# Attention over 128 heads on one core: a block of K in one load of 64 KB rows, its scores in a rolled loop of eight turns

## The chip, the cores and the metric

The kernel runs on one core of a Trainium2 chip. The metric is device time in microseconds (us) of one execution of the whole program. The engines of a core that matter here are TensorE (PE, with its weight loads listed apart as PEld), VectorE (DVE), ScalarE (ACT), GpSimd (POOL) and SyncE (SP); in this kernel SP does nothing but wait and issue DMAs. Each engine runs its own stream of instructions in order, and they meet through semaphores: an instruction adds to one when it ends, and another engine waits until it has reached a value.

## The reference

```python
B, H, Sq, Skv, Dh = 8, 16, 16, 2048, 256      # all bfloat16
scale  = q.shape[-1] ** -0.5
scores = einsum('bhqd,bhkd->bhqk', q, k) * scale
attn   = softmax(scores, axis=-1)
out    = einsum('bhqk,bhkd->bhqd', attn, v)
```

There are B*H = 128 independent heads, each with 16 queries and 2048 keys and values of 256 numbers. K and V are 134 MB each and are read once; queries and output are 1 MB each.

## The kernel before

**Blocks and slots.** The heads are worked off in G = 16 blocks of 8 heads. A block's K is 8 MB and so is its V: 128 partitions, each with 128 tokens of 512 bytes. One SBUF tensor SL holds four slots of 64 tokens a partition (32 KB): VA and VB together hold the V of a block (VW), KA and KB hold K. A half of K (e = 0 or 1, heads 4e to 4e+3) goes to one slot, one load of 4 MB in rows of 32 KB. V comes in one load of 8 MB in rows of 64 KB (L132). Block 0 has its K in VA and VB, since V is not there yet.

**One block.** TensorE contracts over partitions, so K must stand with its features on them. DVE does that in place, 32x32 blocks at a time, by STREAM_TRANSPOSE at L200 (`kt`): four instructions a block, each over 32 tokens. PE then computes scores (`qk`, L302): for each half e and each pair of 512-column banks, eight feature pairs, one weight load of QW for two matmuls of 512 columns; the second matmul of a pair (L297) uses the weights already loaded. These 64 matmuls a block stand written out in the program. DVE takes the row maximum (L222), ACT the exponential (L282), DVE transposes the probabilities (L226, L227), DVE and ACT copy them into the zero-padded weights PTz (`copies`), and PE multiplies them with V (`pv`, L317): 128 weight loads and 128 matmuls of 256 columns. PE's order is: scores of block r, `SPARE` idle matmuls into X_ps (L297), then `pv` of block r-1. ACT also prepares QW of the next block (`qwb`, L256).

**Rolled and written-out loops.** `nc.Fori` makes a loop in the program: the engine's own sequencer computes addresses and wait values in registers and branches back. The loop over blocks is one on every engine. On PE, inside it, everything is written out except the idle matmuls (L354). The scores of block 0 alone are rolled (L328 to L337): a turn of the inner loop has two weight loads and four matmuls of 512 columns, with addresses taken from registers.

**Who releases what.** SP's order of DMA issues is fixed: K half 0 of block j, K half 1 of block j, V of block j-1. A K half is issued when the scores have used up the slot it goes to (c_qk, L150), V when `pv` of the block before has finished with VW (c_pv, L131). The last two blocks load V in pieces (PIECES), each as `pv` frees its rows. GpSimd works only at the start: it sets zeros and spreads the queries (L184).

Of the kernel before, what the change touches and what calls it, by code (L numbers as in the profile page):

```python
# [5 lines left out]
ALU = mybir.AluOpType  # L6
# [4 lines left out]
SP = mybir.EngineType.SP  # L11
BF16 = mybir.dt.bfloat16
# [3 lines left out]
SPARE = 5  # L16
VA, VB, KA, KB = 0, 1, 2, 3
# [3 lines left out]
def bass_standalone__softmax_full_bidir__sampling_kernel(  # L21
# [16 lines left out]
    ku = k.rearrange("b h s d -> (b h s) d").rearrange("(u p t) d -> u p t d", p=128, t=T)  # L38
# [4 lines left out]
    with ExitStack() as es:  # L43
        ec = es.enter_context
        SL = ec(nc.sbuf_tensor("SL", [128, 4, T, D], BF16))
        QT = ec(nc.sbuf_tensor("QT", [128, SQ * D], BF16))
        QW = ec(nc.sbuf_tensor("QW", [128, 2, 128, 8], BF16))

# [8 lines left out]
        O_all = ec(nc.sbuf_tensor("O_all", [128, G + 2, D], BF16))  # L57
# [8 lines left out]
        def sem(name):  # L66
# [4 lines left out]
        s_k = [sem("s_ka"), sem("s_kb")]  # L71
        s_kl = [sem("s_kla"), sem("s_klb")]
        s_v = sem("s_v")
        s_v0 = sem("s_v0")
# [6 lines left out]
        c_kt = [sem("c_kt0"), sem("c_kt1")]  # L81
# [10 lines left out]

        SLf = SL[:].bitcast(F32)

        QX = PTz[:, 1, 0:SQ * D // 128, :].rearrange("p t m -> p (t m)")

        QXu = QX.rearrange("p (c u a y) -> p a u c y", u=8, a=4, y=2)

        QTu = QT[:].rearrange("p (c u y) -> p u c y", u=32, y=2)

        SLk = SL[:].rearrange("p s (c t) (b i q) -> p s c b q t i", t=16, i=32, q=2)


        PIECES = {last - 1: [(0, 60), (60, 39), (99, 29)],
                  last: [(0, 28), (28, 32), (60, 23), (83, 16), (99, 11), (110, 8), (118, 5), (123, 5)]}

        s_p = {a: sem("s_p%d" % a) for a in sorted({a for w in PIECES for a, n in PIECES[w][1:]})}
        VW = SL[:, VA:VB + 1, :, :].rearrange("p a t d -> p (a t) d")


# [9 lines left out]
        def qx(Q, a):  # L120

            return (QTu[32 * a:32 * a + 32, 8 * Q:8 * Q + 8, :, :].rearrange("p u c y -> p c u y"),
                    QXu[32 * Q:32 * Q + 32, a, :, :, :].rearrange("p u c y -> p c u y"))

        def load_k(eng, g, e, slot, t0, n, s):
            eng.dma_start(SL[:, slot, t0:t0 + n, :], ku[2 * g + e, :, t0:t0 + n, :]).then_inc(s, 16)  # L126

        def on_sync(eng):
            def load_v(w, a, n):

                eng.wait_ge(c_pv, 8 * w + (a + n + C - 1) // C)  # L131
                eng.dma_start(VW[:, a:a + n, :], vb[w, :, a:a + n, :]).then_inc(s_p[a] if a else s_v, 16)  # L132

            eng.dma_start(QX, qh).then_inc(s_q, 16)
            for g, s0, s in ((0, VA, s_k0), (1, KA, s_k)):
                for e in range(2):
                    load_k(eng, g, e, s0 + e, 0, T, s[e])

            for e in range(2):
                eng.wait_ge(c_qk, 4 * e + 4)  # L140
                eng.dma_start(VW[:, T * e:T * e + T, :], vb[0, :, T * e:T * e + T, :]).then_inc(s_v0 if e else s_v, 16)
            for e in range(2):
                eng.wait_ge(c_qk, 4 * e + 12)
                load_k(eng, 2, e, KA + e, 0, T, s_k[e])
            for e in range(2):
                eng.wait_ge(c_pv, 4 * e + 12)
                eng.dma_start(VW[:, T * e:T * e + T, :], vb[1, :, T * e:T * e + T, :]).then_inc(s_v0 if e else s_v, 16)
            with nc.Fori(3, last, engines=[SP], hint_back_edge=True) as j:
                for e in range(2):
# [3 lines left out]
            for e in range(2):  # L153
                eng.wait_ge(c_qk, 8 * last + 4 * e - 4)
                load_k(eng, last, e, KA + e, 0, T // 2, s_k[e])
                load_k(eng, last, e, KA + e, T // 2, T // 2, s_kl[e])
# [4 lines left out]
            eng.dma_start(oh[:, 0:last, :], O_all[:, 2:G + 1, :]).then_inc(s_st, 16)  # L161
            eng.wait_ge(c_ev, G + 1)
            eng.dma_start(oh[:, last, :], O_all[:, G + 1, :]).then_inc(s_st, 16)
            eng.wait_ge(s_st, 32)

        def on_gpsimd(eng):

            for x, n in ([(c_pv, 8)] + [(x, 1) for x in s_kl] +
                         [(s_p[a], 16 * G - 16 * sum(a in dict(PIECES[w]) for w in PIECES)) for a in s_p]):
                eng.sem_inc(x, n)  # L170
            eng.memset(QW[:].rearrange("p e m x -> p (e m x)").bitcast(F32), 0.0).then_inc(c_qt, 1)
            zero = [PTz[:, e].rearrange("p t c -> p (t c)").bitcast(F32) for e in range(2)]
            eng.memset(zero[0], 0.0).then_inc(c_pool, 1)
            eng.memset(mk[:], 1.0).then_inc(c_mk, 1)
            eng.memset(P_sb[:, 0:16], 0.0).then_inc(c_mk, 1)
            eng.memset(P_sb[:, 2064:2080], 0.0).then_inc(c_mk, 1)
            eng.wait_ge(c_mk, 3)
# [10 lines left out]
            eng.wait_ge(c_mk, 7)  # L188
            eng.memset(zero[1], 0.0).then_inc(c_pool, 1)

        def on_vector(eng):
# [6 lines left out]
            def kt(e, h, slot, n=1, first=False):  # L198
# [197 lines left out]
```

## Time and profile before

| | |
|---|---|
| time, median of 3 runs | 631.54 us (631.35 to 631.55) |
| span of the profiled execution, first to last instruction | 630.1 us |
| moved by DMA | 270.54 MB, 429 GB/s over the span |
| busy share of the DMA queue's packets | 99.9% of 16 engines' span |
| busy PE, DVE, ACT, POOL | 535.6, 419.4, 269.1, 26.0 us |
| mean granted TensorE clock | 0.976 |

The profiled execution's own time is its span, 630.1 us; the median of the runs is 1.4 us above it. Times in the profile are counted from the span's start. The busy time of PE counts matmuls that overlap in its pipeline more than once, so 85% does not say that PE has 15% left. A row of the timeline is start, length, engine, line, operation, names, and in brackets the idle time before and what ended it. "PEldq" is the sequencer of PE: its rows (FUSED_REGOPS, several register operations in one instruction; ALU_OP, one; COMPARE_BRANCH, the end of a loop) are not counted as busy, but the view of one source line lists how often each ran and its least, median and greatest length in ns.

### The profile page before, as it was taken

Reading aid. Unit: us, or ns where it says so; the run is one execution under the profiler, and the core shown is the slowest. Engines: PE = TensorE matmul, PEld = TensorE weight load, DVE = VectorE, ACT = ScalarE, POOL = GpSimd, SP = SyncE. Lnnn points to the kernel's source line nnn. Section 1 sums busy time; section 2 is a strip of 40 time slices with the busy share of each in tenths; the row PEclk is TensorE's granted clock in tenths of the full one; section 3 lists DMA queues with packets and bytes.
Section 4 is the critical chain, followed back from the end, with each engine's and each line's share of the span. In section 5 each row is a group of like instructions: output and inputs, shape, how many; then the busy total and the mean of one; then the engine's idle time right before and its main releaser. Section 6 shows DMA issues by size and latency. Waiting matters only on the chain.

```text
span 630.1 us, 7710 instructions
## 1 busy us (share of the span) xinstructions
PE 535.6 (85%) x3336; PEld 273.4 (43%) x2561; DVE 419.4 (67%) x193; ACT 269.1 (43%) x308; POOL 26.0 (4%) x30
## 2 busy tenths in 40 slices
PE   1658989889888898888978889888889878899997
PEld 0112734518244272542726336263362724518386
DVE  1989694865849657496574956749566594768740
ACT  1016562723437243362534525335263352732653
POOL 7800000000000000000000000000000000000000
PEclk9998989999899998999999899999998999999999
DMA  9999999999999999999999999999999999999999
GB/s 377 433 435 431 433 431 424 433 439 426 466 399 466 408 433 441 424 441 424 437 453 408 458 408 458 416 424 441 424 441 449 408 458 408 458 404 421 435 428 376
DMA packets 11008, 270.54 MB, mean 429 GB/s; under 512 B 1024, under 2 KB 3072, under 8 KB 3584
## 3 DMA queue, kind: packets, MB, share of 16 engines
q1 hardware_dynamic: 11008, 270.54, 99.9%
HBM read 269.48 MB, written 1.05 MB: 429 GB/s over the span
## 4 chain that ended last, share of the span: by engine, by line
DMA 57%; PE 34%; issue 4%; DVE 4%; SPq 0%; DVEq 0%; ACT 0%
DMA SL<-in_v_dram 52%; PE O_ps L317 30%; DMA SL<-in_k_dram 5%; DVE SL L200 2%; PE S_ps L296 1%; PE S_ps L297 1%; DVE PTb L227 1%; DVE negm L222 1%; PE X_ps L297 1%; SPq L132 0%; DVE PTz L207 0%; DVE PTz L209 0%; SPq L126 0%; ACT P_sb L282 0%; DVE O_all L247 0%
## 5 line engine op out<-in xcount | busy, mean ns | idle before, releaser
L200 DVE STREAM_TRANSPOSE SL<-SL 128x4096 f32<-128x4096 f32 (+1 forms) x63 | 280.6, 4492 | 88.1 <-DMA SL<-in_k_dram 87.6
L296 PE MATMUL S_ps<-SL,QW 128*128 128x512 bf16 (+1 forms) x512 | 206.1, 403 | 57.6 <-DVE SL L200 48.9
L317 PEld LDWEIGHTS O_ps<-SL,PTz 128*128 128x128 bf16 x2048 | 198.9, 98 | 114.2 <-issue 89.0
L317 PE MATMUL O_ps<-SL,PTz 128*128 128x256 bf16 x2048 | 226.6, 273 | 24.9 <-DMA SL<-in_v_dram 23.8
L297 PE MATMUL S_ps<-SL,QW 128*128 128x512 bf16 (+1 forms) x512 | 205.6, 401 | 0.0
L296 PEld LDWEIGHTS S_ps<-SL,QW 128*128 128x128 bf16 (+1 forms) x512 | 74.4, 145 | 230.1 <-issue 161.9
L256 ACT ACTIVATE QW<-QT 32x256 bf16 x64 | 26.9, 420 | 168.5 <-PE S_ps L297 167.3
L269 ACT ACTIVATE PTz<-PTa 16x1024 bf16<-16x1024 bf16 x32 | 33.8, 1056 | 128.9 <-PE O_ps L317 114.2
L222 DVE TENSOR_REDUCE negm<-S_ps 128x1 f32<-128x2048 f32 x16 | 36.6, 2289 | 58.3 <-PE S_ps L297 58.3
L269 ACT ACTIVATE PTz<-PTa,mk 32x1024 bf16<-32x1024 bf16 x64 | 72.3, 1130 | 0.0
L269 ACT ACTIVATE PTz<-PTb 16x1024 bf16<-16x1024 bf16 x64 | 67.2, 1051 | 1.2
L226 DVE STREAM_TRANSPOSE PTa<-P_sb 128x2048 bf16<-128x2048 bf16 x16 | 37.0, 2312 | 35.4 <-ACT P_sb L282 35.4
L297 PE MATMUL X_ps<-QT,QW 128*128 128x512 bf16 x260 | 58.2, 379 | 0.0
L227 DVE STREAM_TRANSPOSE PTb<-P_sb 128x2080 bf16<-128x2080 bf16 x16 | 36.8, 2302 | 0.0
L269 ACT ACTIVATE PTz<-PTb,mk 32x1024 bf16<-32x1024 bf16 x32 | 36.2, 1132 | 0.0
L282 ACT ACTIVATE P_sb<-S_ps,negm 128x2048 bf16<-128x2048 f32 x16 | 31.5, 1967 | 5.9 <-DVE negm L222 5.9
L262 ACT ACTIVATE O_all<-O_ps,rinv 128x256 f32 x15 | 7.1, 473 | 39.8 <-PE O_ps L317 39.8
L184 POOL COPY QT<-PTz 32x1024 bf16<-32x1024 bf16 x16 | 17.4, 1087 | 2.4 <-DVE PTz L194 1.5
L207 DVE TENSOR_SCALAR PTz<-PTb,mk 32x1024 bf16<-32x1024 bf16 x32 | 15.2, 476 | 0.0
L209 DVE COPY PTz<-PTa 16x1024 bf16<-16x1024 bf16 x32 | 13.5, 422 | 1.1
L247 DVE TENSOR_SCALAR O_all<-O_ps,rinv 128x256 bf16<-128x256 f32 x1 | 0.5, 484 | 20.4 <-PE O_ps L317 20.4
L296 PE MATMUL S_ps<-PTz 128*128 128x512 bf16 x1 | 0.6, 608 | 9.9 <-ACT QW L256 9.9
(18 smaller groups left out, 21.0 us busy)
## 6 DMA issues: line engine op xcount, KB each, us to landing
SL<-in_k_dram SPq DMA_DIRECT2D x30, 4096.0 KB, 24.2
SL<-in_v_dram SPq DMA_DIRECT2D x4, 4096.0 KB, 21.3
SL<-in_k_dram SPq DMA_DIRECT2D x4, 2048.0 KB, 21.5
SL<-in_v_dram SPq DMA_DIRECT2D x1, 3840.0 KB, 21.3
SL<-in_v_dram SPq DMA_DIRECT2D x1, 2496.0 KB, 22.0
SL<-in_v_dram SPq DMA_DIRECT2D x1, 2048.0 KB, 12.2
SL<-in_v_dram SPq DMA_DIRECT2D x1, 1856.0 KB, 24.7
SL<-in_v_dram SPq DMA_DIRECT2D x1, 1792.0 KB, 10.8
```

Source lines behind the costliest of these rows:

```text
L184: eng.tensor_copy(*qx(n // 4, n % 4)).then_inc(c_cq, 1)
L200: eng.transpose(x, x).then_inc(c_k0 if first else c_kt[e], n)
L207: ins = eng.tensor_scalar(out=dst, in0=src, scalar1=m, scalar2=None, op0=ALU.mult)
L222: eng.tensor_reduce(out=negm[:], in_=S_ps[:].rearrange("p c n -> p (c n)"), axis=AX.X, op=ALU.max, negate=True).then_inc(c_mx, 1)
L226: eng.transpose(fa[:, 0:2048], P_sb[:, 16:2064]).then_inc(c_pt, 1)
L227: eng.transpose(fb[:, 0:2080], P_sb[:, 0:2080]).then_inc(c_pt, 1)
L256: eng.activation(dv, src(a), ACTF.Copy, scale=scale).then_inc(c_qw, 1)
L269: eng.activation(dst, src, ACTF.Copy, scale=m if x else 1.0).then_inc(c_co[e], 1)
L282: eng.activation(P_sb[:, 16:2064], sv, ACTF.Exp, bias=negm[:], scale=1.0, accum_out=lsum[:]).then_inc(c_ex, 1)
L296: return eng.matmul(dst, w, x, start=start, stop=stop, skip_group_check=not check)
L297: return eng.add_instruction(mybir.InstMatmult(name=nc.get_next_instruction_name(), engine=PE, start_tensor_calc=start, stop_tensor_calc=stop,
L317: ins = eng.matmul(O_ps[:, 0:D], PTz[:, t // T, t % T, :], VW[:, t, :], start=(t == 0), stop=(t == 2 * T - 1))
```

## The change

**Loads.** K of a block stands in one region KW of 128 tokens. Blocks 2 to 13 load it with one DMA of 8 MB in rows of 64 KB; blocks 1 and 14 in a load of tokens 32 to 127 and one of tokens 0 to 31, block 15 in four loads of 32 tokens. Behind KW lies a new region KX of MV = 32 tokens. In blocks 1 to 14 GpSimd copies tokens 0 to 31 of KW to KX (L200), so that tokens 32 to 127 and then 0 to 31 stand in one row of 128 tokens (KS).

**Scores.** DVE transposes 16 tokens at a time (eight instructions a block instead of four). PE's scores are a rolled loop of eight turns; a turn takes 16 tokens, all 16 combinations of half and feature pair, each with a weight load of its own and one matmul of 256 columns. QW and the scores are laid out to suit. K of block j is issued when six of the eight turns of block j-1 have been counted (c_qk at 8j - 2) and the copy to KX has ended (c_x).

**The rest.** The idle matmuls (three times four now) stand ahead of the scores and wait for K (s_k). ACT prepares QW after the exponential instead of before it. Half of the second copies (`copies(1, (2, 3))`) goes from ACT to DVE, and DVE's first copies stand behind all transposes of the next block. V of block 0 is one load behind all scores of block 0. `pv` takes the tokens in the order 32 to 127, 0 to 31. O_all loses two rows, and QT the columns of block 0.

```diff
+MV = 32
-SPARE = 5
+SPARE = 3
...
+        VW, KW, KX = SL[:, 0:2 * T, :], SL[:, 2 * T:4 * T, :], SL[:, 4 * T:4 * T + MV, :]
+        VS, KS = split(VW), split(SL[:, 2 * T + MV:4 * T + MV, :])
...
-            with nc.Fori(3, last, engines=[SP], hint_back_edge=True) as j:
-                for e in range(2):
-                    eng.wait_ge(c_qk, 8 * j + 4 * e - 4)
-                    load_k(eng, j, e, KA + e, 0, T, s_k[e])
+            with nc.Fori(2, last - 1, engines=[SP], hint_back_edge=True) as j:
+                eng.wait_ge(c_qk, 8 * j - 2)
+                eng.wait_ge(c_x, j)
+                load_k(eng, j, KW, 0, 2 * T, s_k)
                 load_v(j - 1, 0, 2 * T)
...
+            eng.wait_ge(c_qk, 8 * last - 2)
+            eng.wait_ge(c_x, last)
+            for t, x in ((32, s_k), (64, s_kb), (96, s_kc), (0, s_kx)):
+                load_k(eng, last, KW, t, 32, x)
...
+            with nc.Fori(1, last, engines=[POOL]) as n:
+                eng.wait_ge(c_qk, 8 * n)
+                eng.wait_ge(s_k, 16 * n)
+                eng.wait_ge(s_kx, ((n + 2) & 16) + 16)
+                eng.sem_inc(c_mk, 1)
+                eng.tensor_copy(KX.rearrange("p t d -> p (t d)"),
+                                KW[:, 0:MV, :].rearrange("p t d -> p (t d)")).then_inc(c_x, 1)
...
-                    ins = mm(S_ps[:, c, :], QW[:, e, :, bp], SLk[:, slot, c, bp // 2, bp % 2, :, :],
-                             e == 0 and bp == 0, e == 1 and bp == 7, c == cs[0])
+            def qk(dst, x):
+                for e in range(2):
+                    for bp in range(8):
+                        ins = mm(dst, QW[:, e, bp, :], x[:, :, bp // 2, 16 * e:16 * e + 16, bp % 2],
+                                 e + bp == 0, e == 1 and bp == 7, True)
...
-                    for e in range(2):
-                        for h in range(2):
-                            eng.wait_ge(c_kt[e], 2 * r + h - 1)
-                            if e + h == 0:
-                                eng.wait_ge(c_ex, rr)
-                            ins = qk(e, (2 * h, 2 * h + 1), KA + e)
-                        ins.then_inc(c_qk, 4)
+                    with nc.Fori(0, 8, engines=[PE]) as i:
+                        eng.wait_ge(c_qw, 4 * r + 4)
+                        eng.wait_ge(c_kt, 8 * r + i - 7)
+                        qk(S_all[:, bass.ds(256 * i, 256)], KS[:, bass.ds(16 * i, 16)]).then_inc(c_qk, 1)
```

On PE, at the scores of a block, the program before has these rows, from the head of the loop over blocks on ("ISA" is one fused register operation of the sequencer; the last two rows alternate on to 64 matmuls):

```order
L340 BRANCH_PREFETCH_HINT
L340 ISA
L343 COMPARE_AND_BRANCH
L346 ISA
L296 MATMUL S_ps<-SL,QW 128x512 [waits c_ex,c_kt0]
L297 MATMUL S_ps<-SL,QW 128x512
```

and at the same place the changed program has these, a whole turn, but for the further pairs of ISA and MATMUL, all alike, that are left out at the dots:

```order
L370 ISA
L372 ISA [waits c_qw]
L323 ISA [waits c_kt]
L323 ISA
L323 MATMUL S_ps<-SL,QW 128x256
...
L370 REGISTER_ALU
L370 COMPARE_AND_BRANCH
```

So 64 matmuls with constant addresses become eight turns of 16 matmuls, each matmul behind one register instruction: 19 ISA rows, one REGISTER_ALU and one branch a turn.

On SP, in the loop over blocks, the rows before are

```order
L126 ISA [waits c_qk]
L126 DMA SL<-in_k_dram 128x16384
L131 ISA
L132 ISA [waits c_pv]
L132 DMA SL<-in_v_dram 128x32768
```

(the two rows of a K half stand there twice), and in the changed program

```order
L132 ISA [waits c_x,c_qk]
L132 DMA SL<-in_k_dram 128x32768
L138 ISA
L139 ISA [waits c_pv]
L139 DMA SL<-in_v_dram 128x32768
```

One K issue with two waits takes the place of two issues with a wait each; V still stands behind K.

More of the change, by code (lines that the diff above doesn't have):

```diff
@@ L11 @@
 SP = mybir.EngineType.SP
+POOL = mybir.EngineType.Pool
 BF16 = mybir.dt.bfloat16
@@ L145, in on_sync @@
[L145 to L156 removed]
+                load_k(eng, 0, VW, T * e, T, s_k0[e])
@@ L289, in on_scalar @@
                     evac(g + 1)
-                copies(1, (0, 1, 2, 3))
+                copies(1, (0, 1))
         def on_tensor(eng):
@@ L316, in pv @@
                         eng.wait_ge(s_p[t], rr)
-                    ins = eng.matmul(O_ps[:, 0:D], PTz[:, t // T, t % T, :], VW[:, t, :],
+                    ins = eng.matmul(O_ps[:, 0:D], PTz[:, t // T, t % T, :], VW[:, (t + MV) % (2 * T), :],
                                      start=(t == 0), stop=(t == 2 * T - 1))
```

200 lines of the change are left out of this document (107 added, 93 removed).

## The prediction

> **What bounds the kernel now.** I read the page's first line, its queue line and its issue lines first, then the chain that ended last, then SP's timeline.
>
> ```profile
> span 630.1 us, 7710 instructions
> q1 hardware_dynamic: 11008, 270.54, 99.9%
> SL<-in_k_dram SPq DMA_DIRECT2D x30, 4096.0 KB, 24.2
> PTz<-in_q_dram SPq DMA_DIRECT2D x1, 1024.0 KB, 5.0
> out_dram<-O_all SPq DMA_DIRECT2D x1, 64.0 KB, 1.6
> ```
> ```profile
> 505.22 24.23 DMA SL<-in_v_dram
> 529.45 0.23 issue
> 529.68 14.15 PE O_ps L317 x128
> 543.99 24.24 DMA SL<-in_v_dram
> ```
> ```profile
> 505.22 0.33 SPq L132 DMA_DIRECT2D SL<-in_v_dram  x1
> 515.02 8.99 SPq L126 DMA_DIRECT2D SL<-in_k_dram  x2
> 543.99 0.33 SPq L132 DMA_DIRECT2D SL<-in_v_dram  x1
> ```
>
> The 16 DMA engines carry packets all the time: the transfers are the bound. A block's round, V issue to V issue, is 543.99 - 505.22 = 38.77 us for 16.8 MB, so 8 MB take 19.39 us. That is held up only because every issue comes while earlier transfers still run. V lands 24.23 us after its issue, 4.8 more than its own 19.39, and about 1.5 of those are the way to the first byte and from the last (out_dram: 1.6 us for 64 KB, of which 0.15 is transfer; the first load's 5.0 less 2.4 gives at most 2.6). Each K half has more than V: 24.2 us in the page's median against 9.7 of its own. So the question for any change to K is when the issue comes; the rate of rows is second.
>
> **The rows of 64 KB.** Packets are back to back either way, and I can bound what longer rows give from slices that are nearly all K in 32 KB rows (the second and third) against the mixture:
>
> ```profile
> GB/s 377 433 435 431 433 431 424 433 439 426 466 399 466 408 433 441 424 441 424 437 453 408 458 408 458 416 424 441 424 441 449 408 458 408 458 404 421 435 428 376
> ```
>
> 433 and 435 against 433 in a round (16.8 MB in 38.77 us): between half a percent lost and half a percent gained, -3 to +3 us over the run; I take 0. The Trainium skill (DMA: Bandwidth & Descriptors, "Where 436 GB/s comes from") puts the ceiling at 435.2 GB/s; by it a round could fall at most to 38.55 us, an estimate of 3 us gained over the run. The round above is within 0.6% of that, so the page speaks for a small gain at best.
>
> **The moved tokens, DVE and ACT.** The GpSimd copy is 8192 elements a partition, once a block in blocks 1 to 14.
>
> ```profile
> L184 POOL COPY QT<-PTz 32x1024 bf16<-32x1024 bf16 x16 | 17.4, 1087 | 2.4 <-DVE PTz L194 1.5
> L173 POOL MEMSET PTz<- 128x4096 f32 x1 | 3.5, 3515 | 0.0
> L194 DVE STREAM_TRANSPOSE PTz<-PTz 128x2048 f32<-128x2048 f32 x1 | 2.3, 2311 | 5.8 <-DMA PTz<-in_q_dram 5.8
> L200 DVE STREAM_TRANSPOSE SL<-SL 128x4096 f32<-128x4096 f32 x62 | 271.9, 4423 | 87.1 <-DMA SL<-in_k_dram 86.6
> L207 DVE TENSOR_SCALAR PTz<-PTb,mk 32x1024 bf16<-32x1024 bf16 x32 | 15.2, 476 | 0.0
> ```
>
> It costs 3.5 us (a memset of the same bytes) to 8.7 (8 x 1087 ns); I take 8.7, the nearer operation. It starts when K has landed and is wanted after six transposes of 2.31 us, 13.9 us later: hidden, with 5 us over, and if that cover went the excess would be paid each block. Eight transposes of 2.31 are 18.5 us where four of 4.42 were 17.7; with four more copies of at most 0.48 DVE has about 2.7 us more a block, in the wait for K, which in this trace is 87 us in all. ACT gives up as many copies: no cost. SP's second wait (c_x) is met 11 us before its first. V of block 0 as one load waits for all scores of block 0, but the loads ahead of it keep the queue full until about 44 us (5.0 for the queries, then 2 x 19.39): no cost.
>
> **The rolled scores.** This is the step that I think decides. The scores of block 0 are rolled in the kernel before, so the trace has a price. PE's timeline, then the sequencer's rows by source line from 28.4 to 42.9 us (ten turns), then the loop of the idle matmuls (L354):
>
> ```profile
> 28.92 0.44 PE L296 MATMUL S_ps<-SL,QW 128*128 x1 [0.35 <-issue]
> 29.19 0.38 PE L297 MATMUL S_ps<-SL,QW 128*128 x1
> 29.41 0.38 PE L296 MATMUL S_ps<-SL,QW 128*128 x1
> 29.63 0.38 PE L297 MATMUL S_ps<-SL,QW 128*128 x1
> 30.33 0.44 PE L296 MATMUL S_ps<-SL,QW 128*128 x1 [0.32 <-issue]
> ```
> ```profile
> L296 PEldq FUSED_REGOPS  x30: 102/138/143, 28.5 to 42.2; - x30
> L296 PEldq ALU_OP  x10: 36/36/36, 29.2 to 42.4; - x10
> L300 PEldq FUSED_REGOPS  x20: 51/51/51, 28.9 to 42.5; - x20
> L330 PEldq FUSED_REGOPS  x10: 50/50/50, 28.4 to 41.6; - x10
> L330 PEldq ALU_OP  x10: 32/32/32, 29.5 to 42.6; - x10
> L330 PEldq COMPARE_BRANCH  x10: 76/208/215, 29.6 to 42.7; - x10
> L354 PEldq ALU_OP  x5: 36/36/36, 403.9 to 405.6; - x5
> L354 PEldq COMPARE_BRANCH  x5: 79/220/222, 404.0 to 405.7; - x5
> ```
>
> A turn takes 30.33 - 28.92 = 1.41 us, though its four matmuls start 0.22 us apart, 0.88 in all: PE waits for "issue", its own sequencer. The nine register rows of a turn last 2 x 0.138 + 0.12 (the third row of L296, between its least and its median) + 2 x 0.051 + 0.050 + 0.036 + 0.032 + 0.208 = 0.82 us; the other 0.59 are gaps, 0.066 a row, two weight loads and four matmuls inside. The changed turn has 21 such rows: 4 at its head (50, 51, 138 and some 41 ns by their like), 15 of 51, one of 36, one branch of 208, in all 1.29 us, and 21 gaps of 0.066 are 1.39: 2.67 us. It also has 16 weight loads and not 2 for every 9 rows, 11 too many for that gap. They cost 0 to one gap each (0.73 us). So a turn is 2.67 to 3.40 us; the rows do not separate the ends, and I take the middle, 3.0. PE itself would want 16 x 0.11 = 1.77 (14.15 us for 128 pairs at L317), and DVE hands over a chunk every 2.31. The sequencer becomes the slowest of the three.
>
> The Trainium skill (TensorE: Matmul & The Clock Gate, "Wait — 56ns, not 53.3ns?") says that with hardware decode off the sequencer spends about 62 ns on each MATMUL. The idle loop does not agree: four matmuls and two register rows take some 0.41 us there, and the two rows with their gaps are 0.036 + 0.22 + 0.13 = 0.39 of it.
>
> **What the turns delay.** K of the next block is now issued after the sixth turn. The way from one turn's last matmul to the issue is in these rows:
>
> ```profile
> 398.12 0.38 PE L297 MATMUL S_ps<-SL,QW 128*128 128x512 bf16 x1
> ```
> ```profile
> 398.68 8.99 SPq L126 DMA_DIRECT2D SL<-in_k_dram  x2
> ```
>
> 0.56 us; with 256 columns some 0.5. From K's landing to the next K's landing: first chunk transposed 2.4; six turns of 3.0 less 0.6 for the rows at a turn's edge that lie before the first wait and after the last matmul, 17.4; to SP 0.5; to the first byte and from the last 1.5; transfer 19.4. Sum 41.2 against 38.8: the queue runs dry and 2.4 us are lost in each of the 12 rounds from K of block 2 to K of block 14, some 29 us. The point at which the round is no longer lengthened is a turn of 2.6 us (38.8 = 23.2 + 6 x 2.6). V's issue also comes late (scores end 26.4 after K's landing, pv 14.15 later, 41 in all) but within the longer round, so it costs nothing beside.
>
> ```profile
> 99.14 4.32 PE X_ps L297 x20
> 627.21 0.05 issue
> ```
>
> The end: V of block 0 lands at 64 (44 + 19.4 + the way) and K of block 2 at 83.7, if its issue just meets the queue's end; I estimate so, and a us later there is a us in the result. Eleven rounds of 41.2 bring K of block 13 to 536.9; issue of K of block 14 20.3 later, its first 96 tokens land 16 us on, at 573.2. Scores of 14: 2.4 + 24. Idle matmuls 12 x 0.216 (4.32 us for 20) = 2.6, pv of 13 14.15, scores of 15 another 24 (their K is long there): 640.3. The first rows of V of block 15 are free after 32 tokens of pv, 3.5; then 1.5 + 19.4 for its pieces, and 2.9 from the last landing to the end (627.2 to 630.1): 667.6. Plus 1.4 from span to median: **669 us**. For the ends, 2.67 gives 639 and 3.40 gives 704 by the same sum.
>
> **Rivals.**
> 1. The register rows are hidden (the sequencer gets ahead while PE still works, or a weight load covers them). Then turns follow the transposes, K's round is 2.4 + 5 x 2.31 + 1.8 + 0.5 + 1.5 + 19.4 = 37.1, under 38.8, and the time stays at 631, give or take the 3 us of the row length. For it: no row shows 16 loads each behind a register row, so the sum of single rows may be too much. Against it: the issue gaps at every turn of the rolled loop quoted.
> 2. Faster: the turn is below 2.6 us and the rows of 64 KB gain over half a percent of the transfer; it takes 1.3 us of its 3 to be outside 0.2%, which is about what a measurement of this kernel tells from no change. 629. Against it: 433 and 435 with short rows already.
> 3. The turn lies only just above 2.6: 633 to 638, from two or three hundredths of a us a row.
> 4. GpSimd's copy takes over 14 us, if it and DVE's transposes hinder each other; DVE then waits, and each us over some 20 (where six slow turns end, and SP waits for c_x) adds 12 us: at 22 us, 690. No row shows the two together.
> 5. Every matmul also costs the sequencer a gap of 0.066: a turn of 3.0 + 1.06, and 12 x 6 + 16 turns of 1.06 more than the forecast, 762. The idle loop speaks against it, as said. This is the direction of the rule of the Trainium skill's page on TensorE named above.
>
> **How the numbers follow.** The forecast (a turn of 2.67 to 3.40, 639 to 704) 0.66; rival 1 0.16; rival 2 0.06; rival 3 0.05; rival 4 0.04; rival 5 0.03. Slower: 0.66 + 0.05 + 0.04 + 0.03 = 0.78; same 0.16; faster 0.06. Predicted is the forecast's 669, its own range 639 to 704. The range for 8 in 10 leaves out rival 2, 4 and 5 in part and the forecast's far end, and takes in rival 1: 630 to 692.
>
> **What would show it.** Right: matmuls at L323 in steady blocks start some 0.13 to 0.16 us apart, turns 3.0 us, with idle put down to issue; the DMA share falls to about 94% and the mean rate to some 405 GB/s (270.54 MB in 668 us); V and K land about 21 us after their issue, since nothing is ahead of them; DVE's transposes end before the turns; POOL shows 14 copies of some 8.7 us ending before their transposes. Wrong: turns of 2.3 to 2.4 that wait for DVE, a DMA share that stays at 99.9%, K landing over 23 us after its issue; or POOL copies over 14 us with DVE waiting on them.

## The result: 680.5 us, 7.7% slower

The changed kernel takes 680.5 us (median of 5 runs, 677.65 to 681.13) beside 631.43 us for the kernel before on the same chip (5 runs, 631.19 to 631.55): a ratio of 1.0769, 95% interval 1.0754 to 1.0785. The forecast was 669.0. The profiled execution has a span of 677.7 us, 47.6 more than before.

Lines of the page after; the first of the groups is the score matmuls (L323), the second the new GpSimd copy:

```profile
span 677.7 us, 12610 instructions
...
DMA  8998999999989999899989998998999999999968
GB/s 371 464 402 371 433 414 391 402 398 429 422 348 410 402 406 433 371 429 375 422 383 433 426 379 371 433 433 371 429 375 422 398 418 387 406 398 437 414 254 303
...
q1 hardware_dynamic: 8992, 270.54, 95.2%
...
L323 PE MATMUL S_ps<-SL,QW 128*128 x1984 | 279.3, 286 | 86.1 <-issue 48.8
...
L200 POOL COPY SL<-SL 128x8192 bf16<-128x8192 bf16 x14 | 98.2, 7015 | 465.5 <-DMA SL<-in_k_dram 465.5
...
L280 ACT ACTIVATE QW<-QT 32x256 bf16 x60 | 80.3, 1338 | 1.1
```

The bytes are the same, the DMA share fell from 99.9% to 95.2%, and the eights in the DMA line stand all along the span: the loss is paid round by round. SP's timeline, where each row is the issue of one transfer (the line L132 loads K, L139 loads V):

```profile
397.06 0.33 SPq L132 DMA_DIRECT2D SL<-in_k_dram  x1
417.37 0.33 SPq L139 DMA_DIRECT2D SL<-in_v_dram  x1
438.26 0.33 SPq L132 DMA_DIRECT2D SL<-in_k_dram  x1
458.53 0.33 SPq L139 DMA_DIRECT2D SL<-in_v_dram  x1
479.24 0.33 SPq L132 DMA_DIRECT2D SL<-in_k_dram  x1
```

A round from K issue to K issue is 41.2 and 41.0 us here, 41.5 in the mean of all twelve (64.69 to 562.99), where the round was 38.77. The issue list of the trace, with the median time to landing, says that almost nothing is queued ahead of a transfer any more (both were 24.2):

```profile
SL<-in_v_dram SPq DMA_DIRECT2D x14, 22.7
SL<-in_k_dram SPq DMA_DIRECT2D x12, 22.0
```

And the chain that ended last shows what the K issue waits for: turns of 16 matmuls, each followed by 0.61 to 0.67 us in which TensorE's own sequencer is between turns, and then the load of K:

```profile
430.15 2.23 PE S_ps L323 x16
432.38 0.61 issue
432.99 2.23 PE S_ps L323 x16
435.22 0.67 issue
435.88 2.22 PE S_ps L323 x16
...
438.26 21.75 DMA SL<-in_k_dram
```

A turn is 432.99 - 430.15 = 2.84 us. By the issue rows of V of block 2 and V of block 13 (117.60 and 543.99 us before, with the end at 630.1; 126.31 and 583.29 after, with the end at 677.7) the 47.6 us fall into three parts: 8.7 up to the first of the two, 30.6 in the eleven rounds between them (41.54 against 38.76), and 8.3 behind the second.

### The profile page after: what moved, and what is told of

It is laid out like the page before. It is cut to its first block, busy times and chain, and to the rows that moved or that the text cites. A ratio compares the mean times of both kernels' runs of the same rounds, so it can differ in the third digit from the quotient of the medians.

```text
span 677.7 us, 12610 instructions
## 1 busy us (share of the span) xinstructions
PE 552.0 (81%) x4212; PEld 391.0 (58%) x4032; DVE 447.3 (66%) x315; ACT 257.7 (38%) x240; POOL 122.5 (18%) x43
## 3 DMA queue, kind: packets, MB, share of 16 engines
q1 hardware_dynamic: 8992, 270.54, 95.2%
## 4 chain that ended last, share of the span: by engine, by line
DMA 47%; PE 23%; DVE 18%; issue 11%; DVEq 0%; SPq 0%; ACT 0%; ACTq 0%
DMA SL<-in_k_dram 47%; DVE SL L212 17%; PE S_ps L323 16%; PE O_ps L347 6%; PE X_ps L324 0%; DVE PTa L241 0%; SPq L132 0%; DVE PTb L242 0%; DVEq L264 0%; DVEq L257 0%; DVEq L265 0%; DVE O_all L271 0%; ACT O_all L287 0%; SPq L145 0%; ACTq L287 0%
## 5 line engine op out<-in xcount | busy, mean ns | idle before, releaser
L323 PE MATMUL S_ps<-SL,QW 128*128 x1984 | 279.3, 286 | 86.1 <-issue 48.8
L212 DVE STREAM_TRANSPOSE SL<-SL 128x2048 f32<-128x2048 f32 (+1 forms) x120 | 278.0, 2382 | 102.3 <-DMA SL<-in_k_dram 102.3
L323 PEld LDWEIGHTS S_ps<-SL,QW 128*128 128x128 bf16 x1984 | 191.7, 97 | 247.6 <-issue 184.3
L200 POOL COPY SL<-SL 128x8192 bf16<-128x8192 bf16 x14 | 98.2, 7015 | 465.5 <-DMA SL<-in_k_dram 465.5
L280 ACT ACTIVATE QW<-QT 32x256 bf16 x60 | 80.3, 1338 | 1.1
L294 ACT ACTIVATE PTz<-PTa,mk 32x1024 bf16<-32x1024 bf16 x32 | 36.2, 1131 | 0.0
L294 ACT ACTIVATE PTz<-PTb 16x1024 bf16<-16x1024 bf16 x32 | 33.5, 1048 | 0.4
L221 DVE COPY PTz<-PTb 16x1024 bf16<-16x1024 bf16 x32 | 13.5, 421 | 4.7 <-PE O_ps L347 3.7
L189 POOL COPY QT<-PTz 32x1024 bf16<-32x1024 bf16 (+1 forms) x16 | 15.7, 981 | 3.1 <-DVE PTz L206 2.1
L219 DVE TENSOR_SCALAR PTz<-PTa,mk 32x1024 bf16<-32x1024 bf16 x32 | 15.2, 476 | 0.0
## 6 DMA issues: line engine op xcount, KB each, us to landing
SL<-in_v_dram SPq DMA_DIRECT2D x1, 3840.0 KB, 17.9
```

What stands on the lines that cost most here:

```text
L200: eng.tensor_copy(KX.rearrange("p t d -> p (t d)"), KW[:, 0:MV, :].rearrange("p t d -> p (t d)")).then_inc(c_x, 1)
L212: eng.transpose(x, x).then_inc(s, n // 16)
L219: ins = eng.tensor_scalar(out=dst, in0=src, scalar1=m, scalar2=None, op0=ALU.mult)
L280: eng.activation(dv, src(a).rearrange("p e (q b) y -> p e q b y", b=4), ACTF.Copy, scale=scale).then_inc(c_qw, 1)
L294: eng.activation(dst, src, ACTF.Copy, scale=m if x else 1.0).then_inc(c_co[e], 1)
L323: return eng.matmul(dst, w, x, start=start, stop=stop, skip_group_check=not check)
```

## The experiments

The theory to be tested: a rolled turn of 2.84 us on TensorE's sequencer, together with one load of K that can only be issued behind the sixth turn, empties the DMA queue. Each ratio is to the kernel before on the same chip (medians of 631.27 to 631.48 us in the four sets). Every time is a median, with the lowest and highest run in brackets.

### One half undone at a time

The turns written out, everything else left:

```diff
-                    with nc.Fori(0, 8, engines=[PE]) as i:
-                        eng.wait_ge(c_qw, 4 * r + 4)
-                        eng.wait_ge(c_kt, 8 * r + i - 7)
-                        qk(S_all[:, bass.ds(256 * i, 256)], KS[:, bass.ds(16 * i, 16)]).then_inc(c_qk, 1)
+                    eng.wait_ge(c_qw, 4 * r + 4)
+                    for i in range(8):
+                        eng.wait_ge(c_kt, 8 * r + (i - 7))
+                        qk(S_all[:, 256 * i:256 * i + 256], KS[:, 16 * i:16 * i + 16]).then_inc(c_qk, 1)
```

> Only the form of the score loop goes back: the eight turns of a block are written out with constant addresses; K stays one load of 64 KB rows, the GpSimd copy stays, DVE still transposes 16 tokens at a time. Theory (the rolled turn of 2.84 us on PE's sequencer makes the round too long): without register rows a turn takes 16 x 0.11 = 1.8 us and follows the transposes of 2.2 us; landing to K issue falls from 19.3 us to about 15.3, a K round would be 37.0 us, below the 38.8 of the transfers, the queue stays full: 630 to 636 us. Rival B (one load for the whole of K is issued and waited for too late, whatever the turns): K issues stay 41 us apart, 670 to 681 us. Rival C (packets of 64 KB are slower, 2498 ns in the mean against 2 x 1210): V and K still land 21.8 us after issue with nothing ahead of them, over 650 us. Rival D (the copy and the 16-token transposes hold DVE up): over 650 us with DVE late in each block.

641.75 us (637.34 to 644.25), ratio 1.0183 [1.0167, 1.0200]. 38.8 us of the 49 come back, so the rolled form was needed for the loss, and rival B as the whole cause falls; C and D were to give over 650 us and fall too. But 10 us stay, 6 more than the theory allowed. (The traced run is the fastest of the five, 637.34 us: what is read from this trace below covers the first 6 of the 10 us.) The number of register rows at L323 on TensorE's sequencer, after and here:

```profile
L323 PEldq FUSED_REGOPS  x2108: 42/46/94, 19.8 to 644.6; - x192
```
```profile
L323 PEldq FUSED_REGOPS  x68: 46/46/80, 19.9 to 36.0; - x68
```

The other half, on SP: turns stay rolled, K of a block comes in three loads.

```diff
-            with nc.Fori(2, last - 1, engines=[SP], hint_back_edge=True) as j:
-                eng.wait_ge(c_qk, 8 * j - 2)
-                eng.wait_ge(c_x, j)
-                load_k(eng, j, KW, 0, 2 * T, s_k)
-                load_v(j - 1, 0, 2 * T)
+            for j in range(2, last):
+                eng.wait_ge(c_x, j)
+                eng.wait_ge(c_qk, 8 * j - 4)
+                load_k(eng, j, KW, MV, 64, s_k)
+                eng.wait_ge(c_qk, 8 * j - 2)
+                load_k(eng, j, KW, MV + 64, 32, s_kc)
+                load_k(eng, j, KW, 0, MV, s_kx)
+                load_v(j - 1, 0, 2 * T)
```

> The opposite half: the turns stay rolled (2.84 us each), but K of a block comes in three loads: tokens 32 to 95 are issued after the fourth turn, 96 to 127 after the sixth, 0 to 31 right behind them (SP's list is written out, with constant waits). Theory: the turn hurts only by way of the issue that waits for the sixth turn. Now the first 64 tokens are issued 2.7 + 4 x 2.84 - 0.5 = 13.6 us after they landed, while 9.7 us of K and V are still queued; the queue stays full and the round is 38.8 us: 631 to 640 us (the last scores and the idle matmuls still cost some us at the end). PE has 22.7 + 14.15 + 0.7 = 37.6 us of work in a round, just under 38.8. Rival F (PE is itself the bound with the rolled turns, through V's issue behind pv): rounds stay at 41 us, 665 to 681 us.

644.05 us (643.80 to 644.52), ratio 1.0202 [1.0186, 1.0217]: 36.5 us come back with every turn still at 2.84, and the time is 4 us above the theory's range. So neither half does the whole harm alone. Two rows of V's issue in SP's timeline, eleven rounds apart:

```profile
122.45 0.33 SPq L139 DMA_DIRECT2D SL<-in_v_dram  x1
...
548.46 0.33 SPq L139 DMA_DIRECT2D SL<-in_v_dram  x1
```

38.73 us a round: rival F (TensorE as the bound) falls. The 12.9 us that the span still has over before lie outside these rounds: 4.85 ahead of the first row, nothing between, 8.4 behind the second. If that reading holds, it must be enough to write out the turns of blocks 1, 14 and 15:

```diff
+                    mid = eng.to_reg((r + 14) & 15)
+                    with eng.If_lt(mid, last - 3):
+                        with nc.Fori(0, 8, engines=[PE]) as i:
...
+                    edge = eng.to_reg((r + 2) & 15)
+                    with eng.If_lt(edge, 4):
+                        eng.wait_ge(c_qw, 4 * r + 4)
+                        for i in range(8):
...
```

> The split load with rolled turns, but the turns of blocks 1, 14 and 15 written out; blocks 2 to 13 stay rolled at 2.84 us a turn. Theory: with K issued after the fourth turn the rolled turns cost nothing in steady rounds (38.85 us there), and the 12.7 us that the split form lost lie at the start (4.8 us at the second V issue) and in the tail (8 us, two blocks of scores of some 22 us in a row with nothing to hide them): 631 to 635 us. If the rolled turns cost in the steady rounds too: over 640 us.

634.53 us (634.40 to 635.43), ratio 1.0049 [1.0034, 1.0065], within the expected range. Twelve blocks of rolled turns cost almost nothing once K's issue does not wait for six of them (V's rounds are 38.85 us, from 118.43 to 545.81); the start and the end, where nothing hides them, cost 9.5 us.

### Doses

Four of the eight turns rolled:

```diff
-                    with nc.Fori(0, 8, engines=[PE]) as i:
+                    with nc.Fori(0, 4, engines=[PE]) as i:
...
+                    for i in range(4, 8):
+                        eng.wait_ge(c_kt, 8 * r + (i - 7))
+                        qk(S_all[:, 256 * i:256 * i + 256], KS[:, 16 * i:16 * i + 16]).then_inc(c_qk, 1)
```

> A dose: the first four turns of a block stay rolled, the last four are written out. Theory: turns 4 and 5 take 1.8 us each instead of 2.84 (their transposes are done by then), so landing to K issue is 2.7 + 11.4 + 3.6 + 0.15 = 17.8 us instead of 19.3 and the round 39.5 instead of 41.1: 0.7 us lost in each of 12 rounds in place of 2.75, plus a shorter end (two blocks of scores 3 to 4 us shorter each): 636 to 648 us, between the written-out and the rolled form. If instead any register loop in the block throws away the same time (a fixed price for entering it): as in the rolled form, over 665 us. If rows hide: no different from the written-out form.

653.55 us (651.86 to 655.21), ratio 1.0355 [1.0335, 1.0375]: between the two forms as the theory has it, 5.5 us above its range.

Every second weight load left out of the rolled turns:

```diff
-                                  e + bp == 0, e == 1 and bp == 7, True)
+                                  e + bp == 0, e == 1 and bp == 7, bp % 2 == 0)
```

> Rolled as in the changed kernel, but every second weight load is left out (its matmul uses the weights of the one before, so the scores are other numbers): 16 register rows and 16 matmuls stay, 8 loads go. It prices what a load costs the sequencer. Theory (the rows set the pace, a load adds about 0.02 us as the raw starts show): the turn falls by 0.15 to 0.2 us to 2.65 to 2.7, K's round by six of these to some 40.0: 662 to 668 us. Rival (each load costs a gap like a row's, 0.066 us): the turn falls by 0.53 to 2.3, below 2.6, and the queue stays full: 635 to 642 us.

671.09 us (666.93 to 674.02), ratio 1.0616 [1.0575, 1.0657], 3 us above the theory's range. Starts of two turns that follow each other in TensorE's timeline:

```profile
422.21 0.28 PE L323 MATMUL S_ps<-SL,QW 128*128 x1 [0.61 <-issue]
...
424.92 0.28 PE L323 MATMUL S_ps<-SL,QW 128*128 x1 [0.66 <-issue]
```

A turn of 2.71, 0.13 less for eight loads: 0.016 us a load. The rival's 0.066 is out, so it is the register rows, those of the turn's edge above all, that set the pace: in the changed kernel the first and the last of a turn's 16 matmuls start 1.95 us apart, where 15 x 0.11 would be 1.65, and from the last start to the next turn's first are 0.89. Of the 1.07 us that a turn has over 16 x 0.11 = 1.77, 0.3 lie between the pairs and 0.8 at the edge.

Four turns of 32 tokens, so that one register row stands for a matmul of 512 columns:

```diff
-                    with nc.Fori(0, 8, engines=[PE]) as i:
+                    with nc.Fori(0, 4, engines=[PE]) as i:
                         eng.wait_ge(c_qw, 4 * r + 4)
-                        eng.wait_ge(c_kt, 8 * r + i - 7)
-                        qk(S_all[:, bass.ds(256 * i, 256)], KS[:, bass.ds(16 * i, 16)]).then_inc(c_qk, 1)
+                        eng.wait_ge(c_kt, 8 * r + 2 * i - 6)
+                        qk(S_all[:, bass.ds(512 * i, 512)], KS[:, bass.ds(32 * i, 32)]).then_inc(c_qk, 2)
```

> The changed kernel, still rolled and with one load of K, but in four turns of 32 tokens (matmuls with 512 columns) in place of eight of 16: half the register rows a token. Theory (register rows are paid per matmul): a turn is 16 x 0.216 = 3.46 us of TensorE, more than 16 pairs at 0.124, so rows inside a turn are hidden and only its edge, some 0.6 us, shows: 4.1 us for 32 tokens, below the 4.4 of their two transposes. K is issued after the third turn: 4.5 (two transposes) + 2 x 4.4 + 3.5 + 0.15 = 17 us after the landing if the clock holds, a round of 38.8; but TensorE idles some 4 us before K lands, so the clock may be at 0.5 for the first turn (as in the written-out form), some 2 us a round: 633 to 655 us. If the loop itself (a turn's head and branch), not the rows per matmul, made it slow: some 2.84 + 1.77 = 4.6 us a turn, 660 us or more.

655.18 us (653.95 to 657.86), ratio 1.0390 [1.0371, 1.0410], at the upper end. The price a token is as expected: the turns now wait for DVE and start 4.39 us apart, though they are still a loop.

```profile
418.14 3.64 PE L323 MATMUL S_ps<-SL,QW 128*128 x16 [0.39 <-DVE SL L212]
422.53 3.64 PE L323 MATMUL S_ps<-SL,QW 128*128 x16 [0.74 <-DVE SL L212]
426.92 3.64 PE L323 MATMUL S_ps<-SL,QW 128*128 x16 [0.75 <-DVE SL L212]
```

### The clock, a second theory

In the written-out form TensorE stands idle 5.2 us before K lands, and the idle matmuls that follow run slowly. The first row here is of TensorE's timeline. The last two are stretches of the round before it, where the gap was 5.16 us: length, busy us of PE, PEld, DVE, ACT and POOL with the number of instructions, granted clock (1.00 is full speed), DMA share, GB/s. The granted clock is 0.50 in the first stretch and 1.00 in the second.

```profile
437.71 4.26 PE L324 MATMUL X_ps<-QT,QW 128*128 128x512 bf16 x12 [5.20 <-DMA SL<-in_k_dram]
```
```profile
398.80:402.00 3.20, 3.12 (x8) 0.00 (x0) 3.20 (x2) 0.88 (x1) 2.87 (x1) 0.50 0.76 328
403.60:418.30 14.70, 14.44 (x129) 12.00 (x127) 14.61 (x11) 0.00 (x0) 2.55 (x1) 1.00 0.99 428
```

That the clock halves when TensorE idles is what the Trainium skill says (TensorE: Matmul & The Clock Gate, "HAM oscillation — how this bites in real kernels": idle gaps of more than about 3.4 us between bursts of matmuls), and the trace agrees at 5.2 us. The theory was that this made up the missing 10 us. The written-out form with 24 idle matmuls that don't wait for K:

```diff
-                    with nc.Fori(0, SPARE, engines=[PE]) as x:
+                    with nc.Fori(0, 2 * SPARE, engines=[PE]) as x:
                         eng.wait_ge(c_cq, 16)
-                        eng.wait_ge(s_k, r16)
                         spare()
```

> The written-out form again, with the idle matmuls no longer waiting for K: 24 of them (for 12) run straight behind the matmuls with V and fill the 5.2 us in which TensorE stood idle before K landed. Theory (of the 10.4 us that the written-out form still lost, most is the clock: after 5.2 us of idleness the granted clock was 0.50, the 12 idle matmuls took 4.3 to 5.3 us instead of 2.75 and turn 0 came 2 to 2.5 us after its chunk was ready): the clock stays at 1.00, turn 0 follows its transpose 2.4 us after the landing, K is issued 15 to 16 us after the landing, the queue is never dry, rounds are 38.8 us: 631 to 635 us. Rival (64 KB packets are slower by themselves: 425 GB/s at a DMA share of 99.4%): no change from the written-out form, 637 to 644 us.

639.16 us (634.72 to 645.88), ratio without the run of 645.88 1.0111 [1.0083, 1.0140]. The mean granted clock rose from 0.930 to 0.979, and at best a quarter of the 10 us was won; the runs of the two forms overlap. The two profiles say why: from DVE's first transpose of K to the next K's issue were 15.8 us cold and are 15.4 warm, because written-out turns of 1.8 us catch up on transposes of 2.2. The theory fell for this form. The rival's number came true; that 64 KB packets are slower by themselves did not, as the section on the seam shows.

The same edit in the rolled form, first with 12 idle matmuls, then with 20:

```diff
                         eng.wait_ge(c_cq, 16)
-                        eng.wait_ge(s_k, r16)
                         spare()
```

> The changed kernel with one edit: the 12 idle matmuls no longer wait for K and run straight behind the matmuls with V (a gap of some 1.8 to 2.1 us before K lands). It prices the clock's part in the rolled form. Theory: the rounds of 42.1 to 42.5 us (idle matmuls at a granted clock of about 0.5, 4.1 to 4.4 us of them) disappear, and the others lose the 0.3 us by which 12 idle matmuls outlast the first transpose: 12 rounds of 40.8 in place of a mean of 41.5, 8 to 9 us less: 670 to 673 us, with less scatter. If the clock has no part in it: 677 to 681 us.

678.75 us (678.47 to 680.49), ratio 1.0750 [1.0734, 1.0765].

```diff
-                    with nc.Fori(0, SPARE, engines=[PE]) as x:
+                    with nc.Fori(0, 5, engines=[PE]) as x:
                         eng.wait_ge(c_cq, 16)
-                        eng.wait_ge(s_k, r16)
                         spare()
```

> The changed kernel with 20 idle matmuls in place of 12, not waiting for K: 4.3 us, which fills the gap before K lands (1.8 to 2.1 us) and the first transpose (2.3 us). With 12 of them nothing was won, since they ended before or soon after the landing and TensorE then stood idle 2.0 to 2.6 us and began the first two turns cold. Theory (the clock has a part of its own in the rolled form): no cold turns, rounds of 40.7 to 41.0 in place of 41.5: 670 to 675 us. If the part of the clock is nothing: 677 to 681 us.

679.68 us (679.42 to 680.53), ratio 1.0769 [1.0753, 1.0786], and with it the granted clock is 0.995 in the mean. Nothing was won that these runs can tell from the changed kernel's 677.65 to 681.13 us: in all three rolled traces first transpose to issue is 19.2 us a round. The timeline of the run with 12 idle matmuls that do not wait for K shows why, in the first four turns of a block:

```profile
380.15 2.64 PE L323 MATMUL S_ps<-SL,QW 128*128 x16 [2.02 <-DVE SL L212]
383.03 5.11 PE L323 MATMUL S_ps<-SL,QW 128*128 x32 [0.23 <-issue]
388.75 2.23 PE L323 MATMUL S_ps<-SL,QW 128*128 x16 [0.61 <-DVE SL L212]
```

Where the matmuls are slow, the gap of 0.61 us behind a turn shrinks to 0.23 or to nothing, and three turns take 388.75 - 380.15 = 8.60 us, where three warm ones take 8.52. So the sixth ends at nearly the same time, and these runs show no part of the clock in the 49 us.

It has one where V is what the round waits for. Both halves undone (the two edits shown first, together), with the idle matmuls where the change puts them:

```diff
-            with nc.Fori(2, last - 1, engines=[SP], hint_back_edge=True) as j:
+            for j in range(2, last):
...
-                    with nc.Fori(0, 8, engines=[PE]) as i:
+                    for i in range(8):
```

> Both halves undone: turns written out, and K in three loads (tokens 32 to 95 after the fourth turn, the others after the sixth). Still changed: 16-token transposes and turns, the GpSimd copy, V of block 0 in one load, the layout of the query weights. Theory (the rest of the change costs nothing): 631 to 634 us, and DMA share 99.8% or more, rounds of 38.8. If copy, transposes or layout cost something by themselves: over 637 us.

641.89 us (640.89 to 642.92), ratio 1.0162 [1.0147, 1.0177], 8 us more than expected. The chain there is V, the matmuls with V, the next V, and a stretch of 3.45 us at their start (columns as above) has half the clock:

```profile
356.70 22.71 DMA SL<-in_v_dram
379.41 0.14 issue
379.55 17.02 PE O_ps L346 x128
```
```profile
379.55:383.00 3.45, 3.45 (x17) 2.47 (x18) 3.30 (x2) 3.40 (x4) 0.00 (x0) 0.50 0.99 427
```

17.02 us for what takes 14.15 at full clock. The idle matmuls taken from ahead of the turns and put back behind them, 20 in blocks 2 to 14:

```diff
-                with eng.If_lt(rr, last):
-                    with nc.Fori(0, SPARE, engines=[PE]) as x:
-                        eng.wait_ge(c_cq, 16)
-                        eng.wait_ge(s_k, r16)
-                        spare()
...
-                    with eng.If_eq(rr, last - 1):
-                        with nc.Fori(0, SPARE, engines=[PE]) as x:
+                    mid = eng.to_reg((r + 14) & 15)
+                    with eng.If_lt(mid, last - 2):
+                        with nc.Fori(0, 5, engines=[PE]) as x:
                             spare()
```

> Split load and written-out turns as in the run that lost 10.6 us, and the 20 idle matmuls of a block put back to where the kernel before has them, behind the scores and ahead of the matmuls with V (none ahead of the scores). Theory: what was left there is the clock alone: with fast scores the place where TensorE waits is in front of V (5.6 to 6.9 us), the matmuls with V then began cold and took 15.6 to 17.0 us in place of 14.15, and the chain V, matmuls with V, next V was that much longer. Filled with 4.3 us of idle matmuls the clock holds: V rounds of 38.8 us, matmuls with V of 14.15, 631 to 634 us. If 16-token transposes, the GpSimd copy, the layouts or loads cost something beside: it stays over 636 us.

634.56 us (634.32 to 634.95), ratio 1.0049 [1.0035, 1.0063]: 7.3 us less. Matmuls with V are at full clock again:

```profile
453.84 14.13 PE L346 MATMUL O_ps<-SL,PTz 128*128 128x256 bf16 x128 [0.26 <-DMA SL<-in_v_dram]
```

So everything else in the change (copy, 16-token transposes, layouts, V of block 0 in one load) costs some 3 us together, 0.6 more than expected; which of it was not tried. By V's issue rows (118.87 for block 2, 545.91 for block 13, a span of 633.6) 1.3 us of the span's 3.5 lie at the start, 0.7 in the eleven rounds and 1.6 in the end. No version run beats the kernel before.

### The copy

GpSimd's copy made twice in a row:

```diff
+                for h in range(2):
+                    eng.wait_ge(c_mk, 6 + (n - 1) + h)
                     eng.tensor_copy(KX.rearrange("p t d -> p (t d)"),
-                                KW[:, 0:MV, :].rearrange("p t d -> p (t d)")).then_inc(c_x, 1)
+                                    KW[:, 0:MV, :].rearrange("p t d -> p (t d)")).then_inc(c_x if h else c_mk, 1)
```

> The changed kernel with GpSimd's copy of the 32 tokens made twice in a row (the second over the first), 14 us in place of 7.0, so that it ends about when the seventh transpose is due, 15 to 16 us after K's landing. Theory (the copy is hidden under six rolled turns, 19.2 us): 678 to 682 us, no change. Rival (copy and transposes hinder each other, or DVE waits for the copy with consequence): each us that the seventh transpose is pushed past turn six adds to the end of the scores and, past 19.2 us, to K's issue: over 684 us, and DVE's transposes beside the copy longer than 2.27 us.

680.59 us (679.77 to 682.17), ratio 1.0787 [1.0769, 1.0805], beside 680.5: no change. The two groups of this trace (by shape):

```profile
L213 DVE STREAM_TRANSPOSE SL<-SL 128x2048 f32<-128x2048 f32 x114 | 253.4, 2280 | 112.4 <-DMA SL<-in_k_dram 94.3 <-POOL SL L201 18.1
...
L201 POOL COPY SL<-SL 128x8192 bf16<-128x8192 bf16 x28 | 196.4, 7013 | 374.5 <-DMA SL<-in_k_dram 373.7
```

DVE now waits 18.1 us for the copies, and it is hidden under the slow turns; transposes beside 14 us of copying take 2280 ns, 2274 in the changed kernel.

### What was missing in the theory: the seam between two transfers

All kernels with one load of K were slower than the sum said. Per round, in us, worked out from the issue rows, from DVE's first transpose of each K, and from the trace's packets. "Packets late" is how much longer than their usual time (2.42 us for 64 KB) the packets of one DMA engine took in a round, "engine empty" how long it had no packet; both are means over the 16 engines. The first six rows are means of the twelve rounds from K of block 2 to K of block 14, the last two of eleven rounds of V:

```
kernel                   issue to     transpose    round    packets   engine
                         transpose    to issue              late      empty
changed                  22.3         19.2         41.5     1.30      1.49
half the loads           22.85        18.35        41.2     1.29      1.30
four turns rolled        22.95        17.3         40.2     0.71      0.81
turns of 32 tokens       23.1         17.3         40.5     0.84      0.92
written out              23.35        15.8         39.2     0.41      0.05
written out, warm        23.9         15.4         39.3     0.54      0.06
split, rolled            (three loads)             38.7     0.0       0
before                   (two loads)               38.8     0.05      0
```

In every row the last two columns together are what the round has over 38.8 us, to within 0.2. So in the changed kernel the empty queue, which was forecast, is about half of the 2.8 us lost in a round; the other half is packets that take longer.

The sum took the round as the greater of 38.8 and 21 + the second column, a sharp corner at 17.9. The corner is round: at 17.3 the round is already 1.5 us too long, at 15.4 0.5, and only with a load issued well ahead does the excess go. Of the late time, 88 to 99% is in packets that start within 3 us of the point where one transfer follows the other. In the changed kernel the first 16 packets of a transfer take 3.1 us in the median (the middle half of them 2.9 to 3.2).

In these traces the lateness goes with how long before the end of the transfer ahead the next one is issued; no run varied that alone. From the same packets, in us, the mean of each kernel's twelve seams of a kind, with the least and the greatest lead:

```
kernel, transfer         issued ahead by      late at the seam
changed, K               0.0 (-1.6 to 0.8)    0.68
changed, V               0.9 (0.8 to 1.0)     0.62
written out, K           1.9 (0.4 to 2.7)     0.30
written out, warm, K     2.2 (1.4 to 2.8)     0.44
turns of 32 tokens, V    3.0 (2.8 to 3.6)     0.13
written out, V           3.5 (2.8 to 3.9)     0.06
```

So what stays of the loss in the written-out form lies at the seam ahead of K, which is issued some 2 us ahead; V, issued 3.5 us ahead, follows with almost none. Why a packet takes longer at the seam was not tried and stays open.

## Why the prediction was right, and where its terms were off

- **The mechanism** is the one forecast: turns set by the sequencer, K's issue behind the sixth, the queue empty, a longer round for each block. Each half undone alone brings 36 to 39 us of the 49 back. The rivals fall: rows hidden, and faster (the turns wait for "issue" and the result is slower); a turn just above the threshold (2.84 against 2.6); the copy (7.0 us, and 14 cost nothing); another gap for each matmul (2.84, not 4.06). On this last the rule of the Trainium skill that it cited (TensorE: Matmul & The Clock Gate, "Wait — 56ns, not 53.3ns?") shows as no further cost a matmul: a pair of load and matmul starts every 0.124 us with its 46 ns row. Whether the 62 ns that the rule names lie within the 0.124 us these runs do not tell.
- **The turn**: 3.0 predicted, 2.84 measured. The middle was taken between loads that cost nothing and loads that cost a gap each; measured, a load costs 0.016 us, a quarter of a gap, so the lower end was nearer: 2.67 and 11 loads at 0.016 make 2.85. Inside a turn the matmuls start 0.124 us apart, where 0.13 to 0.16 was said.
- **K's round**: 41.2 predicted, 41.5 measured, by two errors that cancel, so the close number is luck. From landing to issue the sum had 20.3 (2.4 + 17.4 + 0.5), measured 19.2; from issue to landing it had 20.9, measured 22.3 (both up to and from DVE's first transpose). The second is the mis-sized step from issue to landing. By the packets, the 22.3 are 1.1 to an engine's first packet, 19.4 of transfer, 0.7 of late packets at the seam, 0.8 by which the last of the 16 engines ends behind the middle one, and 0.3 to the transpose: the "1.5 to the first byte and from the last" held, and the late packets and the uneven end were missing beside it. The threshold of 2.6 us worked out from it is therefore not one.
- **The start**: K of block 2 was to land at 83.7 "if its issue just meets the queue's end; a us later there is a us in the result". It did not meet it: V of block 0 ended at 63.30, K of block 2 was issued at 64.69, and no packet ran until 65.65. Its first transpose starts 22.05 us after the issue, at 86.74: 3.0 us too late.
- **The end** was mis-sized by about 5 us. TensorE's timeline of the changed kernel:

```profile
609.14 14.14 PE L347 MATMUL O_ps<-SL,PTz 128*128 128x256 bf16 x128
623.11 1.94 PE L323 MATMUL S_ps<-SL,QW 128*128 x16
...
645.45 14.13 PE L347 MATMUL O_ps<-SL,PTz 128*128 128x256 bf16 x128 [0.46 <-issue]
660.59 14.13 PE L347 MATMUL O_ps<-SL,PTz 128*128 128x256 bf16 x128 [1.00 <-ACT O_all L287]
```

  The sum let the last V's pieces set the end (3.5 + 1.5 + 19.4 + 2.9 = 27.3 from the start of the matmuls with V of block 14). In fact TensorE waits for no V there (the last piece lands at 672.4, its matmuls come at 674.2), and two blocks of matmuls with V run in a row with an evacuation between: 677.7 - 645.45 = 32.2. Together: 3.0 at the start, 4.0 in eleven rounds (41.56 against 41.2), -1.2 from K of block 13 to the issue of the next, 0.9 in that load, -1.5 in the scores and matmuls up to 645.45, 4.9 behind: the 10.1 us between the forecast span of 667.6 and 677.7.
- **The copy**: 8.7 predicted (eight small copies), 7.0 measured, hidden as said. **64 KB rows**: taken as 0, and a packet in the middle of a transfer takes 2.42 us as two of 32 KB took 2.43; what the long single loads cost beside the empty queue is the seam. **DVE and ACT**: hidden as said.

## What to carry to other kernels

A rolled loop with register addresses has a price a matmul (here 0.124 us for a pair that TensorE does in 0.11, plus 0.8 us at a turn's edge), and it shows only where a transfer is issued behind it, or at the start and the end, where nothing hides it: look first at which transfer waits for the loop, and split that transfer, before unrolling. A loop on the sequencer stops setting the pace when each row carries more work (with 512 columns in place of 256 the turns followed DVE, though the kernel was still 3.9% slower than before). When a DMA-bound kernel is summed up, don't take a transfer that is issued just in time as free; count it as late until it is issued well before the one ahead of it ends (here some 3.5 us).

## What the runs showed of the hardware

- **Packets are slower at the seam**: 3.1 us in the median for the first 64 KB packets of a transfer that was issued less than 1 us before the one ahead of it ended (changed kernel), 2.42 in mid-transfer. Issued 3.5 us ahead, the seam lost 0.06 us (written out, V).
- **The clock can fall after a shorter gap than expected.** In the rolled form with 12 idle matmuls ahead of K, TensorE stood idle 2.63 us before 422.18, and the stretch behind has:

```profile
422.20:424.50 2.30, 2.30 (x13) 1.59 (x14) 2.30 (x2) 0.00 (x0) 2.30 (x1) 0.62 1.05 456
```

  The Trainium skill's 3.4 us (TensorE: Matmul & The Clock Gate, "HAM oscillation — how this bites in real kernels") is longer than this gap; the measurement decides: 0.62 is the granted clock behind 2.63 us of idleness.
- **ScalarE's copy of the query weights** takes 1338 ns in the new layout (L280 above). The group in the page of before, for the same 32x256 elements:

```profile
L256 ACT ACTIVATE QW<-QT 32x256 bf16 x64 | 26.9, 420 | 168.5 <-PE S_ps L297 167.3
```

  Three times as long, beside other work; it was not in the prediction, and no run priced it by itself.
